# Layer 1 in pairs (0,1) to (6,7) and block 8 as two half blocks, with an unread weight quarter left unwritten and a ring of seven weight tiles

## The chip, the core and the metric

The kernel runs on one core of a Trainium2 chip. The metric is the device time of the run in microseconds (us); the median of three runs is taken. TensorE (PE) does the matrix products, VectorE (DVE) and ScalarE (ACT) the elementwise work, GpSimd (POOL) almost nothing, and SyncE (SP) issues nearly all transfers (DMA), in the order of its program.

## The reference

4608 tokens of 512 values go through three steps. First a linear attention: for each of 8 batches of 576 tokens and 8 heads, `kv = k^T v`, `out = q kv`, divided by its root mean square and scaled. Then layer 1, a gated feed-forward with an inner width of 1536, and layer 2, one with a squared ReLU and an inner width of 2048:

```python
xn = x / rms(x) * rms_g
h1 = silu(xn @ w_gate) * (xn @ w_val)      # 512 -> 1536
x2 = h1 @ w_out                            # 1536 -> 512
h2 = maximum(x2 @ w_in, 0) ** 2            # 512 -> 2048
out = h2 @ w_out2                          # 2048 -> 512
```

All is float32; the weights arrive as float64.

## The kernel before

**Blocks and stages.** The tokens are cut into 9 blocks of 512 (`T`). `stages` (L341) lists what is worked on together: in layer 1 the blocks (0,1), then (2,) alone, then (3,4), (5,6), (7,8); in layer 2 (0,1) to (6,7) and at last (8,8), which is block 8 as two half blocks of 256 columns (`width`, L100). Each stage has an x part (`x_stage`, L741: the products with w_gate and w_val, or w_in) and an h part (`h_stage`, L848: the products with w_out or w_out2).

**Products.** Each float32 operand is split into a high part (ACT, L624) and a low part (DVE, L625), and a product is three passes of matmuls (`PASSES`, L712). A pair of blocks can go through a scheme with seven products of quarter matrices in place of eight (`run_seven` L963, the second half of `x_stage`), which needs sums of weight quarters (S1 to S4, made once) and sums of the data quarters (T1 to T4: `x_steps` L639, and `forms` L856 with their subtractions L628). The other way is plain (`run_plain` L933, L794). `x_plain` (L344) makes the x part plain in (0,1) and (2,); `h_plain` (L333) makes the h part plain in (0,1), (2,), (3,4). A matmul of L717 (x part), L945 (plain h) or L980 (seven, h) takes a 128x128 weight tile against 512 columns, or 256 in a half-block stage. One product of an x part for one pair of weight tiles is 12 matmuls, six for each half of the pair (`g`); so is one product of an h part (`d`).

**Counts of matmuls.** x part of layer 1: 288 for a plain block, 504 for a pair (or for two half blocks) with seven products. h part of layer 1: 144 for a plain block, 252 for a pair with seven products. Layer 2: 336 and 336 for a pair.

**Weights.** In stage (0,1) the weights are turned from float64 to split float32 and put into DRAM (`prep_unit` L122: `hi` L190, `lo` L201, `put` L211). A tile in DRAM (`wd`) has four quarters of both halves of a pair; the tile h=0 has the quarters 11, 12, 21, 22, the tile h=1 the sums S1 to S4. Units of kind "words" make the h=0 part, units of kind "sums" load the words again (L176) and make the h=1 part, and units of kind "all" (layer 2) make both. Steps of these units stand in `prep_q`; `tick` (L690), called after every six matmuls of an x part, takes `pace["prep"]` of them (L1187). From the second stage on each product loads its weights, 128 x 2 x 2 x 256 float32 = 0.524 MB, into one of the tiles of a ring (`w_fetch` L359, `W_RING` = 5, four more in layer 2). SP issues the next load once the product has given its tile free, so SP goes in step with PE.

**Order.** All instructions stand in an order written out by hand: `after(n, ...)` and `at(t, ...)` put work on a later tick, each engine takes its instructions in that order. Three operand tiles (`hop`) hold the split operands of the h part; `ahead` forms the operand of product n+2 when product n is put out. The queue `xs` (L876 to L918) holds what the next stage's x part needs: loads of x (L668), scaling (layer 1, L674), splits and subtractions, one item per call of `x_next`, which in `run_seven` stands after each six matmuls. `h_result` (L1021) writes the results of layer 1 into tiles `o` of the pool `t` (8 tiles in rotation, L77) and puts them to `x2d` five ticks later. The attention of blocks 2 to 8 is spread over the ticks of layer 1 (`kv_events` L580, `o_events` L586, L764 to L773).

## Time and profile before

| | us |
|---|---|
| median of three runs (1625.38 to 1630.46) | 1626.92 |
| the profiled execution | 1629.3 |
| its span, first to last instruction | 1627.5 |
| PE busy | 1598.4 (98%) |
| DVE busy | 1152.8 (71%) |
| ACT busy | 715.0 (44%) |
| DMA q1, share of 16 engines | 82.3% |

The stages of the profiled execution, read from the chain that ended last: (0,1) to 264.5, (2,) to 381.5, (3,4) to 581.2, (5,6) to 757.4, (7,8) to 930.9, then layer 2 with (0,1) to 1084.2, three more pairs to 1541.2, and (8,8) to 1621.9. The granted clock of TensorE is 0.998 of its full 2.4 GHz in the mean. A busy share near 100% on PE tells that little time is left between matmuls, so what counts is how much work PE has and where it waits.

### The profile page before, as it was taken

The page shows a single profiled execution, that of the slowest core. Times are in us where ns is not written, and L with a number is a line of the kernel's source. Part 1 is how long each engine was busy: PE and PEld are TensorE (multiplying, and loading weights), DVE is VectorE, ACT ScalarE, POOL GpSimd, SP SyncE. Part 2 cuts the span into 40 slices and gives each one's busy share as a digit, 9 for nine tenths or more (in the row PEclk, how much of TensorE's full clock was granted, in tenths as well). Part 3 has the DMA queues.
Part 4 walks back from the last instruction along what each step waited for, and adds up shares of the span by engine and source line. Part 5 has one row for each costly group of instructions (what it writes and reads, how often), then busy time and mean ns, then how long its engine had stood idle before and what let it go on. Part 6 is the DMA issues. An engine that isn't in the chain of part 4 may idle for free.

```text
span 1627.5 us, 21390 instructions
## 1 busy us (share of the span) xinstructions
PE 1598.4 (98%) x8024; PEld 1327.2 (82%) x8024; DVE 1152.8 (71%) x1590; ACT 715.0 (44%) x967; POOL 6.7 (0%) x19
## 2 busy tenths in 40 slices
PE   8899999999999999999999999999999999999998
PEld 7678878777888788788878888888888888888898
DVE  6755675657684767976778688875886588569676
ACT  5543443235553545546554553532353235224433
POOL 0100000000000000000000000000000000000000
PEclk9999999999999999999999999999999999999999
DMA  9885889998997989979997898686678667866797
GB/s 350 284 297 194 274 294 364 381 363 289 365 358 248 351 287 332 367 223 307 356 399 247 286 395 282 222 255 207 196 243 246 196 194 243 244 196 200 225 400 264
DMA packets 176198, 464.92 MB, mean 286 GB/s; under 512 B 14048, under 2 KB 47840, under 8 KB 171744
## 3 DMA queue, kind: packets, MB, share of 16 engines
q1 hardware_dynamic: 175552, 463.30, 82.3%
q8 instruction: 64, 1.05, 0.3%
q10 hardware_dynamic: 544, 0.26, 0.1%
q14 instruction: 38, 0.31, 0.0%
HBM read 356.55 MB, written 106.95 MB: 285 GB/s over the span
## 4 chain that ended last, share of the span: by engine, by line
PE 83%; DMA 6%; DVE 5%; ACT 3%; issue 1%; SPq 0%; POOL 0%; POOLq 0%; ACTq 0%; DVEq 0%
PE c L717 45%; PE a L980 16%; PE e L980 8%; PE acc L945 8%; PE d L980 4%; DMA wt<-wd_g 2%; DMA wd_p<-ws 2%; DMA kvraw<-in_kv_dram 1%; PE ops L448 1%; PE kvps L408 1%; DVE wpw L169 1%; DVE ws L202 1%; ACT ws L199 1%; DVE wpw L163 1%; ACT wpw L157 1%
## 5 line engine op out<-in xcount | busy, mean ns | idle before, releaser
L717 PE MATMUL c<-xo,wt 128*128 128x512 f32 (+1 forms) x3480 | 765.2, 380 | 7.9 <-DMA wt<-wd_g 6.1
L717 PEld LDWEIGHTS c<-xo,wt 128*128 128x128 f32 x3480 | 627.6, 188 | 135.0 <-DMA wt<-wd_g 5.9
L625 DVE TENSOR_TENSOR ho<-hr,ho 128x1024 fp32r<-128x1024 f32 (+1 forms) x212 | 243.0, 1147 | 86.7 <-ACT ho L624 85.8
L624 ACT ACTIVATE ho<-hr 128x1024 fp32r<-128x1024 f32 (+1 forms) x212 | 212.0, 1001 | 184.9 <-PE a L980 85.9
L980 PE MATMUL a<-ho,wt 128*128 128x512 f32 (+1 forms) x1248 | 267.0, 373 | 0.0
L980 PEld LDWEIGHTS a<-ho,wt 128*128 128x128 f32 x1248 | 221.6, 188 | 41.1
L728 ACT ACTIVATE s<-c 128x512 f32<-128x512 f32 (+1 forms) x228 | 127.7, 573 | 175.0 <-PE c L717 174.5
L732 DVE TENSOR_TENSOR c<-c,s 128x512 f32<-128x512 f32 (+1 forms) x174 | 112.8, 649 | 80.2 <-PE c L717 77.2
L717 PE MATMUL c<-xo,ws 128*128 128x512 f32 x576 | 139.8, 398 | 4.3 <-ACT ws L199 3.6
L980 PE MATMUL e<-ho,wt 128*128 128x512 f32 (+1 forms) x624 | 133.5, 373 | 0.0
L717 PEld LDWEIGHTS c<-xo,ws 128*128 128x128 f32 x576 | 106.8, 189 | 28.7 <-ACT ws L199 4.8
L980 PEld LDWEIGHTS e<-ho,wt 128*128 128x128 f32 x624 | 110.8, 188 | 20.6
L628 DVE TENSOR_TENSOR hr<-hr 128x1024 f32<-128x1024 f32 (+1 forms) x104 | 118.5, 1139 | 1.8
L625 DVE TENSOR_TENSOR xo<-xr,xo 128x1024 fp32r<-128x1024 f32 (+1 forms) x58 | 67.0, 1157 | 57.2 <-ACT xo L624 57.2
L945 PE MATMUL acc<-ho,wt 128*128 128x512 f32 x432 | 102.9, 396 | 1.9 <-DMA wt<-wd_o 1.9
L788 DVE TENSOR_TENSOR hr<-c,hr 128x512 f32<-128x512 f32 x108 | 73.8, 685 | 33.4 <-PE c L717 30.8
L945 PEld LDWEIGHTS acc<-ho,wt 128*128 128x128 f32 x432 | 81.4, 191 | 19.5 <-DMA wt<-wd_o 2.3
L202 DVE TENSOR_TENSOR ws<-wpl,ws 128x1024 fp32r<-128x1024 f32 x49 | 59.8, 1220 | 28.9 <-ACT ws L199 28.8
L739 DVE SCALAR_TENSOR_TENSOR hr<-c 128x512 f32<-128x512 f32 (+1 forms) x120 | 76.5, 638 | 3.6
L199 ACT ACTIVATE ws<-wpl 128x1024 fp32r<-128x1024 f32 x49 | 51.7, 1055 | 44.8 <-DVE wpl L188 23.6
L624 ACT ACTIVATE xo<-xr 128x1024 fp32r<-128x1024 f32 (+1 forms) x58 | 57.1, 1002 | 32.0 <-DVE xr L628 32.0
L783 ACT ACTIVATE r<-c 128x512 f32<-128x512 f32 (+1 forms) x40 | 22.1, 554 | 108.1 <-PE c L717 98.5
(81 smaller groups left out, 1148.9 us busy)
## 6 DMA issues: line engine op xcount, KB each, us to landing
wt<-wd_g SPq DMA_DIRECT2D x150, 512.0 KB, 6.8
wt<-wd_i SPq DMA_DIRECT2D x140, 512.0 KB, 5.0
wt<-wd_p SPq DMA_DIRECT2D x140, 512.0 KB, 3.9
wt<-wd_o SPq DMA_DIRECT2D x78, 512.0 KB, 5.1
wd_g<-ws SPq DMA_DIRECT2D x24, 1024.0 KB, 10.0
kvraw<-in_kv_dram SPq DMA_DIRECT2D x32, 512.0 KB, 7.1
wd_i<-ws SPq DMA_DIRECT2D x16, 1024.0 KB, 7.9
wd_p<-ws SPq DMA_DIRECT2D x16, 1024.0 KB, 8.5
```

Source lines behind the costliest of these rows:

```text
L199: nc.scalar.activation(out=st[h][:, :, 0, :], in_=quarters(st["sw"[1 - h]]), func=AF.Copy)
L202: nc.vector.tensor_tensor(out=st[h][:, :, 1, :], in0=quarters(st["sw"[1 - h]]), in1=st[h][:, :, 0, :].bitcast(F32), op=ALU.subtract,)
L624: nc.scalar.activation(out=dst[:, 0], in_=src, func=AF.Copy)
L625: eng.tensor_tensor(out=dst[:, 1], in0=src, in1=dst[:, 0].bitcast(F32), op=ALU.subtract)
L628: eng.tensor_tensor(out=o, in0=x, in1=y, op=ALU.subtract)
L717: nc.tensor.matmul(ps, lhsT=w[:, a, kc * 128:(kc + 1) * 128], rhs=x[:, b, kc, :], start=(start and n == 0 and kc == 0), stop=(n == 2 and k ...
L728: nc.scalar.activation(out=t, in_=ps, func=AF.Copy)
L732: nc.vector.tensor_tensor(out=o, in0=ps, in1=t, op=ALU.add)
L739: nc.vector.scalar_tensor_tensor(out=hr, in0=c, scalar=0.0, in1=c, op0=ALU.max, op1=ALU.mult)
L788: after(2, lambda: nc.vector.tensor_tensor(out=hr, in0=c, in1=hr, op=ALU.mult))
L945: nc.tensor.matmul(acc[c], lhsT=wt[:, a, (c % 2) * 128:(c % 2 + 1) * 128], rhs=x[:, b, e, :], start=(n == 0 and e == 0 and a + b == 0), st ...
L980: nc.tensor.matmul(ps, lhsT=w[e][:, a, d * 128:(d + 1) * 128], rhs=x[:, b, e, :], start=(i in (1, 2, 5) and q == 0 and e == 0 and a + b == 0),
```

## The change

Layer 1 has the stages (0,1), (2,3), (4,5), (6,7) and (8,8), where (8,8) is block 8 as two half blocks, as layer 2 had already. All of them but (0,1) have an x part with seven products; the h part is plain in (0,1) and (2,3). So stage (0,1) now loads and prepares the x of two blocks (2 and 3) and has to finish their attention, whose events are put closer together. In the tiles h=0 the quarters 22 and 21 change places (on the host too), so that 21 is the last; it isn't read by seven products. It is not put to DRAM for w_gate, w_val, w_in and w_out2, and not computed either for the last two (`n_hi`, `n_put`). Two tiles of the pool `sm` join the ring after stage (0,1): seven tiles in layer 1, eleven in layer 2. The units of layer 2's weights are spread as 2, 4, 6, 0 over the stages of layer 1 from (2,3) to (8,8), and 4 in the first stage of layer 2, where it was 4, 3, 6 and 3; seven "sums" units of w_gate and w_val stand in the x part of (2,3), where they stood in that of (2,). A result tile of a half block waits until its other half is there.

```diff
@@ -31,8 +31,8 @@
-PLACE_X = {"11": (0, 0), "12": (0, 1), "21": (0, 2), "22": (0, 3)}
-PLACE_H = {"11": (0, 0), "21": (0, 1), "12": (0, 2), "22": (0, 3)}
+PLACE_X = {"11": (0, 0), "12": (0, 1), "22": (0, 2), "21": (0, 3)}
+PLACE_H = {"11": (0, 0), "22": (0, 1), "12": (0, 2), "21": (0, 3)}
...
@@ -72,7 +72,7 @@
-    smp = ctx.enter_context(tc.tile_pool(name="sm", bufs=1))
+    smp = ctx.enter_context(tc.tile_pool(name="sm", bufs=2))
...
@@ -127,6 +127,7 @@
+        n_hi, n_put = (3 if m in "ip" else 4), (4 if m == "o" else 3)
...
@@ -196,20 +197,23 @@
-            nc.scalar.activation(out=st[h][:, :, 0, :], in_=quarters(st["sw"[1 - h]]), func=AF.Copy)
+            k = 4 if h else n_hi
+            nc.scalar.activation(out=st[h][:, :k, 0, :], in_=quarters(st["sw"[1 - h]])[:, :k], func=AF.Copy)
 
         def lo(h):
+            k = 4 if h else n_hi
             nc.vector.tensor_tensor(
-                out=st[h][:, :, 1, :],
-                in0=quarters(st["sw"[1 - h]]),
-                in1=st[h][:, :, 0, :].bitcast(F32),
+                out=st[h][:, :k, 1, :],
+                in0=quarters(st["sw"[1 - h]])[:, :k],
+                in1=st[h][:, :k, 0, :].bitcast(F32),
...
         def put(h):
-            nc.sync.dma_start(out=wd[pair][h][:, :, e], in_=st.pop(h).bitcast(F32))
+            k = 4 if h else n_put
+            nc.sync.dma_start(out=wd[pair][h][:, :k, e], in_=st.pop(h)[:, :k].bitcast(F32))
...
@@ -331,23 +335,24 @@
     def h_plain(layer, blocks):
-        return len(blocks) == 1 or layer == 1 and blocks[0] < 5
+        return layer == 1 and blocks[0] < 4
-    stages = [(1, (0, 1)), (1, (2,))] + [(1, (n, n + 1)) for n in range(3, NB, 2)]
-    stages += [(2, (n, n + 1)) for n in range(0, NB - 1, 2)] + [(2, (NB - 1, NB - 1))]
+    stages = [
+        (layer, b) for layer in (1, 2) for b in [(n, n + 1) for n in range(0, NB - 1, 2)] + [(NB - 1, NB - 1)]
+    ]
     def x_plain(layer, blocks):
-        return len(blocks) == 1 or (layer, blocks) == stages[0]
+        return (layer, blocks) == stages[0]
...
@@ -603,9 +608,9 @@
-                at(u + 4 + 4 * c, lambda c=c: att_y(j, c, nc.vector))
-                at(u + 6 + 4 * c, lambda c=c: x1_turn(j, c))
-                at(u + 22 + 2 * c, lambda c=c: x1_put(j, c))
+                at(u + 4 + every * c, lambda c=c: att_y(j, c, nc.vector))
+                at(u + 4 + every // 2 + every * c, lambda c=c: x1_turn(j, c))
+                at(u + 4 + every // 2 + every * NQ + every // 2 * c, lambda c=c: x1_put(j, c))
...
@@ -665,7 +668,9 @@
-        nc.sync.dma_start(out=t, in_=x1d[j][k].rearrange("c p t -> p c t") if layer == 1 else x2d[j][:, k, cols])
+        nc.sync.dma_start(
+            out=t, in_=x1d[j][k, :, cols].rearrange("c p t -> p c t") if layer == 1 else x2d[j][:, k, cols]
+        )
...
@@ -756,21 +761,20 @@
             if first[0] and (n, t) == (0, 2):
                 while chain:
                     tick()
                 t0 = now[0] + 1
-                for j in range(stages[1][1][0], NB):
-                    gap, period = (6, 47) if j < 5 else (8, 60)
-                    if j == 2:
-                        kv_events(j, t0, gap)
-                        t0 += 28
-                    o_events(j, t0, 5)
+                kv_events(2, t0, 4)
+                t0 += 18
+                for j in range(2, NB):
+                    gap = 4 if j == 2 else 8
+                    o_events(j, t0, 5, every=2 if j < 4 else 4)
                     if j + 1 < B:
-                        kv_events(j + 1, t0 + 17, gap)
-                    t0 += period
+                        kv_events(j + 1, t0 + 17, 6 if j == 3 else gap)
+                    t0 += (35, 44, 55)[min(j - 2, 2)]
...
@@ -876,20 +880,13 @@
-            if first[0]:
-                at = {"11": (0, "11"), "21": (0, "21")}
-                when = dict.fromkeys(at, 11)
-            elif len(blocks) == 1:
-                at = {"11": (1, "12"), "21": (1, "22"), "12": (2, "12"), "22": (2, "22")}
-                when = dict.fromkeys(at, 0)
-            elif plain:
+            if plain:
                 at = {"11": (1, "11"), "21": (2, "11"), "12": (1, "21"), "22": (2, "21")}
                 when = {"11": len(seq), "21": len(seq), "12": len(seq) + 2, "22": len(seq) + 2}
             else:
                 at = {"11": (1, "11"), "21": (2, "11"), "12": (1, "12"), "22": (2, "12")}
                 when = {"11": 4 * nq, "21": 4 * nq, "12": 5 * nq, "22": 5 * nq}
-            if len(nb) == 1:
-                at = {b: at[b] for b in ("11", "21")}
+
...
@@ -909,11 +906,14 @@
-            t1 = when["11"]
-            load_two(t1, "11", "21", 4 if nl == 1 else 3)
-            xs.extend([step(0, t1), step(1, t1)])
-            if len(nb) > 1:
-                t2 = when["12"]
+            t1, t2 = when["11"], when["12"]
+            if first[0]:
+                xs.extend([load("11"), load("21"), load("12"), load("22")] + [(t2, [])] * 3)
+                xs.extend((t2, [lambda n=n: x_scale(xt[n], n)]) for n in ("11", "21", "12", "22"))
+                xs.extend(step(n, 13 if n > 6 else 11) for n in range(8))
+            else:
+                load_two(t1, "11", "21", 4 if nl == 1 else 3)
+                xs.extend([step(0, t1), step(1, t1)])
                 load_two(t2, "12", "22", 3 if nl == 1 else 2)
                 xs.extend(step(n, t2) for n in range(2, 8))
...
@@ -1013,7 +1013,7 @@
-            if nxt and len(nxt[1]) > 1:
+            if nxt:
                 late.extend([lambda n=n: x_step(n) for n in range(8, 13)])
...
@@ -1022,17 +1022,28 @@
-        j, o = blocks[n], new_tmp("o")
+        j, parts = blocks[n], T // width(blocks)
+        o = o_two.pop(c, None)
+        if o is None:
+            o, whole = tmp.tile([128, T], F32, tag="t", name="o"), parts == 1
+            if not whole:
+                o_two[c] = o
+        else:
+            whole = True
         to = o
         if turned(j):
-            to = o.rearrange("p (i a t) -> p a i t", a=NQ, t=BL)
-            ps, t = (x if x is None else x.rearrange("p (a i t) -> p a i t", a=NQ, t=BL) for x in (ps, t))
+            k = NQ // parts
+            a = slice(n * k, (n + 1) * k) if parts > 1 else slice(0, NQ)
+            to = o.rearrange("p (i a t) -> p a i t", a=NQ, t=BL)[:, a]
+            ps, t = (x if x is None else x.rearrange("p (a i t) -> p a i t", a=k, t=BL) for x in (ps, t))
         if t is not None:
             add(to, ps, t)
         else:
             nc.scalar.activation(out=to, in_=ps, func=AF.Copy)
-        after(5, lambda: nc.sync.dma_start(out=x2d[j][:, c, :], in_=o))
-
+        if whole:
+            after(5, lambda: nc.sync.dma_start(out=x2d[j][:, c, :], in_=o))
...
@@ -1080,24 +1091,25 @@
-            + prep_units([(key, "sums") for key in gv[:N_SUMS]], 6, hops, rooms + [(xop, "x21"), (smp, "sm")] * 2, stgs),
-            prep_units([(key, "sums") for key in gv[N_SUMS:]], 5, hops, xts[:3], stgs + xts[:2:-1]),
+            + prep_units([(key, "sums") for key in gv[:N_SUMS]], 6, hops, rooms + [(smp, "sm", smp, "sm")], stgs),
-        for n, many in enumerate((4, 3, 6, 3)):
+        for n, many in enumerate((2, 4, 6, 0, 4), 1):
             units = l2_units[lo:lo + many]
             lo += many
-            if n == 3:
+            if n == 5:
                 preps.append(units)
                 continue
-            steps = prep_units(units, 11 if many < 5 else 9, hops, hops, stgs, pad=True)
+            steps = prep_units(units, 11 if many < 5 else 9, hops, hops, stgs, pad=True) if many else []
             if n == 1:
+                steps = prep_units([(key, "sums") for key in gv[N_SUMS:]], 4, hops, hops, stgs, pad=True) + steps
+            if n == 2:
                 steps = prep_units(o_sums[3:], 9, hops, hops, stgs, pad=True) + steps
             preps.append(steps)
-        h_preps[2] = prep_units(o_sums[:3], 9, hops, [(xop, "x22"), (xop, "xT4")], stgs, pad=True)
+        h_preps[1] = prep_units(o_sums[:3], 9, hops, [(xop, "x22"), (xop, "xT4")], stgs, pad=True)
...
@@ -1184,7 +1196,7 @@
-            pace["prep"] = 1.0 if n == 0 else len(prep_q) / {1: 40, 4: 70, 5: 40}.get(n, 64)
+            pace["prep"] = 1.0 if n == 0 else len(prep_q) / {1: 62, 2: 66, 3: 70}.get(n, 46)
...
@@ -1196,7 +1208,8 @@
-                for _ in range(W_RING):
+                w_places.extendleft([(smp, "sm")] * 2)
+                for _ in range(len(w_places)):
                     w_fetch()
...
@@ -1216,10 +1229,11 @@
-        return rows(w)
-    def rows(w):
-        return np.ascontiguousarray(w.reshape(-1, 2, 128, DM).transpose(0, 2, 1, 3)).view(np.int64)
+        return rows(w, (0, 1, 3, 2))
+    def rows(w, order=(0, 3, 2, 1)):
+        w = w.reshape(-1, 2, 128, 2, DM // 2).transpose(0, 2, 1, 3, 4).reshape(-1, 128, 4, DM // 2)
+        return np.ascontiguousarray(w[:, :, order, :]).reshape(-1, 128, 2, DM).view(np.int64)
```

## Rows read from the trace of the kernel before

**Rows 1.** The profile page: engine, busy us, share of the span, instructions.
```profile
PE 1598.4 (98%) x8024; PEld 1327.2 (82%) x8024; DVE 1152.8 (71%) x1590; ACT 715.0 (44%) x967; POOL 6.7 (0%) x19
```

**Rows 2.** Waits of PE: line, what it waited for, us in total, times, longest.
```profile
PE c L717 <- DMA wt<-wd_g: 6.1, 6, 1.7
...
PE acc L945 <- DMA wt<-wd_o: 1.9, 1, 1.9
```

**Rows 3.** The chain that ended last, in order of time: start us, us, what.
```profile
554.80 26.37 PE acc L945 x108
...
1236.52 76.16 PE c L717 x336
...
1541.16 40.37 PE c L717 x336
```

**Rows 4.** Stretches of layer 1: us, then each engine's busy us, PEclk, DMA share, GB/s.
```profile
264.50:304.00 39.50, 37.74 (x194) 31.14 (x193) 20.20 (x38) 11.19 (x18) 0.00 (x0) 1.00 1.01 355
304.00:344.00 40.00, 36.68 (x208) 28.49 (x207) 24.26 (x50) 10.60 (x14) 0.00 (x0) 1.00 1.02 378
...
815.00:874.00 59.00, 57.84 (x253) 46.80 (x252) 43.09 (x60) 30.86 (x45) 0.00 (x0) 1.00 0.97 369
```

**Rows 5.** The same view around the wait in the plain h part of (3,4).
```profile
550.00:554.50 4.50, 2.89 (x24) 1.90 (x22) 2.59 (x3) 3.10 (x5) 0.00 (x0) 1.00 1.01 380
554.50:558.00 3.50, 3.20 (x8) 2.52 (x9) 1.89 (x3) 1.54 (x2) 0.00 (x0) 0.56 1.05 413
```

**Rows 6.** The same view over the half-block stage of layer 2: x part, h part.
```profile
1541.00:1581.50 40.50, 40.50 (x339) 40.48 (x338) 27.17 (x65) 14.16 (x36) 0.00 (x0) 1.00 1.03 385
1581.50:1622.00 40.50, 40.37 (x337) 40.16 (x335) 31.21 (x56) 18.66 (x33) 0.00 (x0) 1.00 0.84 305
```

**Rows 7.** PE groups by shape: xcount, busy us, mean ns, idle before.
```profile
L717 PE MATMUL c<-xo,wt 128*128 128x512 f32 x3144 | 724.6, 391 | 7.9 <-DMA wt<-wd_g 6.1 <-DVE hr L732 0.8 <-DVE c L732 0.6
...
L945 PE MATMUL acc<-ho,wt 128*128 128x512 f32 x432 | 102.9, 396 | 1.9 <-DMA wt<-wd_o 1.9
```

**Rows 8.** DMA in the x part of (2,), 264.5 to 344: all, and issues to landing.
```profile
DMA packets 12315, 29.13 MB, mean 366 GB/s; under 512 B 863, under 2 KB 2911, under 8 KB 12309
...
wt<-wd_g SPq DMA_DIRECT2D x19, 512.0 KB, 9.2
wd_g<-ws SPq DMA_DIRECT2D x7, 1024.0 KB, 9.6
```

**Rows 9.** DMA in the x part of (3,4), 381.5 to 508.
```profile
DMA packets 15636, 41.43 MB, mean 328 GB/s; under 512 B 1190, under 2 KB 3824, under 8 KB 15115
```

**Rows 10.** DMA in the x part of (7,8), 757.5 to 874.
```profile
DMA packets 13595, 41.67 MB, mean 358 GB/s; under 512 B 1003, under 2 KB 1003, under 8 KB 12819
```

**Rows 11.** Instructions at the start of (7,8), in order of time.
```profile
760.69 0.61 SPq L1034 DMA_DIRECT2D x2d<-o  x1
```

**Rows 12.** DMA in the h part of (7,8), 874 to 931: us to landing.
```profile
xr<-x2d SPq DMA_DIRECT2D x4, 512.0 KB, 6.2
...
x2d<-o SPq DMA_DIRECT2D x6, 256.0 KB, 6.0
```

**Rows 13.** Instructions in that h part, in order of time: start us, us.
```profile
898.50 1.22 DVE L628 TENSOR_TENSOR hr<-hr 128x1024 f32<-128x1024 f32 x1
...
899.80 2.93 SPq L668 DMA_DIRECT2D xr<-x2d  x2
...
907.06 1.05 ACT L624 ACTIVATE xo<-xr 128x1024 fp32r<-128x1024 f32 x1
...
909.29 1.22 DVE L625 TENSOR_TENSOR ho<-hr,ho 128x1024 fp32r<-128x1024 f32 x1
...
910.42 1.22 DVE L625 TENSOR_TENSOR xo<-xr,xo 128x1024 fp32r<-128x1024 f32 x1
```

**Rows 14.** DVE groups by shape: xcount, busy us, mean ns, idle before.
```profile
L625 DVE TENSOR_TENSOR ho<-hr,ho 128x512 fp32r<-128x512 f32 x28 | 19.1, 684 | 6.4 <-ACT ho L624 5.7
...
L732 DVE TENSOR_TENSOR c<-c,s 128x256 f32<-128x256 f32 x24 | 10.1, 419 | 9.5 <-PE c L717 9.5
```

More of the change, by code (lines that the diff above doesn't have):

```diff
@@ L933, in run_plain @@
         def run_plain():
-            for nb, j in enumerate(blocks):
+            for nb in range(len(blocks)):
                 bk = [banks.popleft() for _ in range(4)]
```

13 lines of the change are left out of this document (6 added, 7 removed).

## The prediction

> **What bounds the kernel now.** The page first: PE is busy for 98% of the span, DVE for 71%, ACT for 44% [rows 1]. So time goes with the work of PE, and with the few waits of PE. The list of waits comes next: 6.1 us for weights of w_gate and w_val and 1.9 us for weights of w_out are the large ones after the start [rows 2]. The chain gives the price of a matmul where nothing disturbs it: 336 with 512 columns in 76.16 us are 226.7 ns each, 336 with 256 columns in 40.37 us are 120.1 ns each [rows 3]. Half the columns cost 53% and not 50%: half-width matmuls pay 6.8 ns more than half a full one. The stretches show where PE waits in layer 1: it lacks 1.76 and 3.32 us in the two halves of the x part of (2,), with the DMA share at 1.01 and 1.02, and 1.16 us in (7,8) at 0.97 [rows 4]. So these waits are for transfers in crowded stretches. One more lies in the plain h part of (3,4): PE is busy for 2.89 of 4.5 us, and in the next 3.5 us the granted clock is 0.56 of full speed, a mix of its two levels, 1.2 and 2.4 GHz [rows 5]. The 108 matmuls from there took 26.37 us in place of 24.5, so this wait of 1.9 us cost 1.9 us more by the clock [rows 2, 3]. The stage whose form the change copies, (8,8) of layer 2, holds PE without a gap while DMA moves 385 GB/s, and its h part has DVE busy for 31.2 of 40.5 us [rows 6].
>
> **PE's work.** Behind stage (0,1), layer 1 has x parts of 288 + 3 x 504 = 1800 and plain and seven h parts of 144 + 288 + 2 x 252 = 936 full matmuls. The groups agree: 3144 - 4 x 336 = 1800, and 432 = 144 + 288 [rows 7]. That is 2736 x 226.7 ns = 620.2 us. After: 3 x 504 + 288 + 2 x 252 = 2304 full ones, 522.3 us, and 504 + 252 = 756 half ones, 90.8 us; sum 613.1. **PE gains 7.1 us.** The attention's matmuls keep their number and only move to earlier ticks.
>
> In the TensorE: Matmul & The Clock Gate page of the Trainium skill (section Back-to-back issue gap) a warm matmul takes N/2.4 + 2.5 ns, 215.8 and 109.2 here; by that the gain would be 10.7 us and the sum 3.6 us lower. The trace disagrees, with 226.7 and 120.1 ns [rows 3].
>
> **The x part of (2,3).** It replaces that of (2,) as the place where seven "sums" units run beside the weight stream. The (2,) part moved 29.13 MB in 79.5 us at 366 GB/s, seven puts of 1.05 MB among them, a weight load landing 9.2 us after its issue [rows 8]. Without its 5.1 us of lacking PE time it would have asked for 392 GB/s. In (2,3): 42 loads x 0.524 = 22.0 MB, sums 7 x (0.524 + 1.049) = 11.0, two "all" units (1.049 in, 0.786 + 1.049 out) 5.8, attention and results about 7 (the 41.43 MB of (3,4) less 43 loads and four units of 3.15 leave 6.3, and blocks now come a little closer) [rows 9]. That is 45.8 MB; the x part of (3,4) took 126.5 us [rows 9], so 364 GB/s, but the sums stand in the first 48 of 84 ticks: 12.6 + 11.0 + 4 MB in some 72 us, 383 GB/s. The ask is the old one, and the two more tiles are 1.05 MB, 2.9 us at 366 GB/s. Bounds for the wait: 2.6 us (5.5, the old one for 72 us, less 2.9) to 6.1 (the ring lends nothing), and 13.6 if the stretch gets only the 328 GB/s of (3,4) [rows 9]. I take 3.5, nearer to the low end because the demand falls behind tick 48 and the ring can refill. **-2.6 us.** Behind a load that waits on SP for its put stand all later loads, puts and attention loads.
>
> **The h part of (2,3)** is that of (3,4) with the same three o units. Its wait of 1.9 + 1.9 us arose because SP put o's weights late; two tiles more are 2 x 2.72 us more lead. **-3.5 us** (0 to -3.8). For the same reason the 1.16 us of (7,8), whose units also write 0.26 MB less each [rows 4]: **-0.9** (0 to -1.2). The unread quarter saves 12 + 16 puts of 0.26 MB and a quarter of 16 `hi` and `lo`; it lies beside PE and I give it no time of its own. If the transfers were the bound it would be 7.3 MB, 20 us at 366 GB/s, against 27 more weight loads (255 for 228), 14.2 MB.
>
> **The x part of the half stage.** 42 loads of 0.524 MB in 60.5 us are 364 GB/s, below the 385 shown [rows 6], with a ring of seven for nine there. I give 0.5 (0 to 5). Then the tiles `o`: the last results of (6,7) are put late, the first of the two at +3.3 us in the old order (760.69, the stage beginning at 757.4) [rows 11], where SP follows a full product; with half products about +1.8. It lands 6.0 us later [rows 12], at 7.8. The tile is wanted by the seventh new tile, the copy of product 5, at 5.8, and PE needs this copy at 7.9: late by some 0.5, and by 3 with a landing of 9 us. I give 1.5. Together **+2** (0 to 6).
>
> **The h part of the half stage**, the largest new term. A product lasts 12 x 120.1 ns = 1.44 us. The next stage's x is full width and its steps stand at fixed counts of products, from product 9 on, so all distances halve. In the old (7,8) the first x load waits for a subtraction of DVE, is issued at 899.80, and its split starts at 907.06, 7.3 us later, more than the 6.2 it takes to land [rows 12, 13]. Counted from the start of product 9, the half stage has the two loads at 0.8 and 2.4, landing at 7.0 and 8.6; the split stands at 4.7. ACT waits, and the form of operand 14 behind it comes too late for product 14, due at 7.2. From 8.1 (7.0 + 1.05 on ACT) DVE still has 7 forms, 4 full splits, 2 full subtractions, 4 half adds. Full ones follow each other in 1.13 us (909.29, 910.42), 0.09 less than they are long [rows 13]; so 0.60 for a form of 0.68 and 0.34 for an add of 0.42 [rows 14]: 4.2 + 6.8 + 1.4 = 12.4. The last operand is there at 20.5, its product ends at 21.9; undisturbed it ends at 17.3. That is 4.7, and 0.5 for handing from ACT to DVE: **+5.2 us**. Low end 1 (loads land in time and the operand tiles cover DVE's surplus), high end 10 (landing 9.2 [rows 8] and once more 1.9 of clock).
>
> **The rest.** The first stage of layer 2 gets four units for three, 2.1 MB more, 5.7 us of transfer at 366 GB/s [rows 8], beside a deeper ring: **+1** (0 to 3). Stage (0,1): SP waits for the put of block 3's x, some 8 us, ahead of the loads of the sums units; DVE gets two splits and two subtractions more. Operands are formed two products (11 us) ahead: **+1** (-1 to 4).
>
> **The sum.** -7.1 - 2.6 - 3.5 - 0.9 + 2 + 5.2 + 1 + 1 = -4.9 us. The profiled run took 1629.3 (span 1627.5), 2.4 above the median of 1626.9; so 1624.4 for such a run and 1622 for the median.
>
> **Rivals.** *Covered*: the loads of x land in time and the ring swallows the waits: -7.1 - 6.1 - 3.8 - 1.2 + 2.4 (DVE's surplus in the half stage) = -15.8, 1611. For it: (8,8) of layer 2 had no wait with DVE at 0.77; against: that stage has no next one. *Transfers bound (2,3)*: at 328 GB/s its 45.8 MB take 139.6 us, 13.6 of waiting for my 3.5, and 1.9 of clock: +7.1 us, 1634. It gives slower from a rate under 333 GB/s on (a wait over 11.5 us). For it: shares of 1.01 and 1.02 in (2,) [rows 4]; against: 366 GB/s there [rows 8], 358 in (7,8) [rows 10]. *The ring does nothing*: crowded transfers are late whatever the depth, 6.1 and 3.8 us stay: +1.2, 1628.
>
> The DMA: Bandwidth & Descriptors page of the Trainium skill (Specifications) states an HBM limit of about 358 GB/s for a core. By that the second rival would hold, (2,3) taking 127.9 us and the 33.0 MB of the half stage 92.3 for 90.8. The trace disagrees, with 385 GB/s over 40 us [rows 6].
>
> **How the numbers follow.** My forecast has a chance of 0.52, with 1616 to 1628 as its own range; covered 0.22; transfers bound 0.18; ring does nothing 0.08. A measurement tells 0.3%, 4.9 us, from no change: below 1622.0 is faster, above 1631.8 slower. Half of the forecast (0.26) and "covered" are faster, 0.48; the other half, the last rival and 0.02 of the third are the same, 0.36; the rest, 0.16, slower. The range reaches from the second case to the third: 1611 to 1634.
>
> **What would show it.** Right: 504 and 252 half-width matmuls of L717 and L980 in layer 1 at 120 ns each, with no gap between them in the x part; waits of ACT or DVE for x from x2d shortly before layer 2, and PE lacking about 5 us there; fewer waits for wt<-wd_o. Wrong: no such lack (then nearer 1611), or PE lacking over 10 us in the x part of (2,3), or in stage (0,1), whose end should lie within 5 us of 264.5 plus the attention moved into it.

## The result and the profile after

| | before | after |
|---|---|---|
| median, us | 1626.94 (1625.38 to 1630.46) | 1645.28 (1643.29 to 1647.51) |
| ratio to before, 95% interval | | 1.0110 (1.0087 to 1.0133) |
| span of the profiled execution, us | 1627.5 | 1645.0 |
| mean granted clock | 0.998 | 0.993 |

The change makes the kernel 18 us slower, against a forecast of 5 us faster. The page of the kernel after: busy us and share of each engine, then the transfers.

```profile
PE 1602.0 (97%) x8348; PEld 1342.5 (82%) x8348; DVE 1183.4 (72%) x1680; ACT 735.7 (45%) x1043; POOL 6.7 (0%) x19
...
q1 hardware_dynamic: 176400, 470.12, 82.4%
...
HBM read 370.71 MB, written 99.61 MB: 286 GB/s over the span
```

PE is busy for 3.6 us more, though its work fell, and the time in which it does nothing grew from 29.1 to 43.0 us [rows 1]. The work did fall as forecast. In the chain of after, the x part of the half stage stands as one piece without a gap:

```profile
842.19 60.47 PE c L722 x504
...
1254.17 76.16 PE c L722 x336
```

That is 120.0 ns for a half matmul, and 226.7 for a full one as before [rows 3]. So the gain of 7.1 us is there, and some 25 us (these 7.1 and the 17.5 by which the span grew) came in elsewhere: 13.9 as idle time of PE, and about 10.7, an estimate from the busy time (3.6 more for 7.1 less), as matmuls that ran longer at a lower clock (0.993 for 0.998 in the mean). The list of waits of PE (what for, us in total, times, longest) says for whom:

```profile
PE c L722 <- ACT s L733: 8.3, 6, 3.0
PE acc L945 <- ACT ws L201: 3.8, 1, 3.8
...
PE a L980 <- ACT ho L629: 2.6, 1, 2.6
PE a L980 <- DVE ho L630: 2.4, 3, 1.0
PE c L722 <- DVE c L737: 2.4, 3, 1.3
PE kvps L413 <- DVE ss L488: 2.2, 1, 2.2
```

No wait of PE for a streamed weight tile (`wt`) is left in it; 6.1 and 1.9 us of those are gone [rows 2]. In their place stand waits for ACT and DVE. The stretches place them (us, then busy us of PE, PEld, DVE, ACT, POOL; PEclk, DMA share, GB/s). After: h part of (0,1); x and h part of (4,5); x part of (6,7); x and h part of the half stage; first x part of layer 2.

```profile
195.50:280.60 85.10, 78.36 (x402) 63.18 (x401) 63.40 (x102) 42.80 (x53) 0.00 (x0) 0.94 0.90 315
...
481.00:607.50 126.50, 123.70 (x594) 101.91 (x593) 99.47 (x163) 66.07 (x102) 0.00 (x0) 1.00 0.94 339
607.50:667.40 59.90, 58.76 (x254) 46.67 (x253) 52.93 (x68) 32.43 (x39) 0.00 (x0) 1.00 0.76 256
667.40:784.90 117.50, 115.29 (x505) 94.27 (x504) 84.32 (x117) 63.98 (x92) 0.00 (x0) 1.00 0.95 344
...
842.00:902.50 60.50, 60.50 (x506) 60.47 (x504) 30.30 (x69) 26.63 (x67) 0.00 (x0) 1.00 0.99 364
902.50:940.60 38.10, 32.97 (x254) 31.95 (x253) 29.12 (x43) 17.67 (x30) 0.00 (x0) 0.96 0.99 363
940.60:1025.50 84.90, 79.33 (x338) 63.79 (x337) 67.80 (x95) 38.27 (x53) 0.00 (x0) 0.98 0.95 349
```

The same view of the kernel before: h part of (0,1), x and h part of the plain (2,), x part of (5,6), first x part of layer 2.

```profile
189.70:264.40 74.70, 74.06 (x410) 59.73 (x409) 55.71 (x87) 37.75 (x46) 0.00 (x0) 1.00 0.91 325
264.40:344.00 79.60, 74.52 (x401) 59.73 (x400) 44.46 (x87) 21.79 (x32) 0.00 (x0) 1.00 1.02 366
344.00:381.50 37.50, 37.50 (x202) 30.98 (x201) 18.39 (x22) 17.76 (x26) 0.00 (x0) 1.00 0.91 325
...
581.20:700.30 119.10, 118.34 (x537) 97.76 (x537) 88.90 (x145) 60.11 (x90) 0.00 (x0) 1.00 0.94 335
...
930.90:1007.90 77.00, 76.72 (x338) 62.88 (x337) 63.01 (x87) 35.23 (x49) 0.00 (x0) 1.00 0.95 353
```

Stage (0,1) ends at 280.6 for 264.5, 16.1 us later. About 4 us of it is attention that moved in: 48 matmuls more on PE in that stage, four steps `ops` and one `kvps` of later blocks. In its h part (85.1 us for 74.7) PE stands idle for 6.7 us where it was 0.6, and the matmuls run at a clock of 0.94 for 1.00. Layer 1 behind it takes 660.0 us for 666.4. The first stage of layer 2 takes 84.9 for 77.0. From there on both kernels take 619 us. 16.1 - 6.4 + 7.9 = 17.6, the growth of the span.

Two places show how PE is held up. First, stage (0,1): DVE's list, then ACT and PE, in the order of time (start us, us, what; in brackets the idle time before it and who ended it).

```profile
219.53 1.18 DVE L164 SCALAR_TENSOR_TENSOR wpw<-wps,wpw 128x1024 int32<-128x1024 int32 x1
220.64 0.68 DVE L541 TENSOR_TENSOR y<-y,r 128x512 f32<-128x512 f32 x1
221.24 1.22 DVE L170 SCALAR_TENSOR_TENSOR wpw<-wps,wpw 128x1024 int32<-128x1024 int32 x1
...
222.49 1.06 ACT L201 ACTIVATE ws<-wpw 128x1024 fp32r<-128x1024 f32 x1 [4.36 <-DVE wpw L170]
223.60 0.50 PE L945 MATMUL acc<-ho,ws 128*128 128x512 f32 x1 [3.82 <-ACT ws L201]
```

L164 and L170 turn the words of a weight that PE needs next; L541 scales the attention's `y` and was written between them, and one more pair of attention steps (L541, L556) ran just ahead, from 218.18 to 219.53. DVE takes its list in order, so ACT gets the weight late and PE stands for 3.82 us. The pair ahead takes 1.35 us and L541 between the two steps 0.60: together about half of the wait. The stretches there:

```profile
219.80:223.60 3.80, 0.00 (x1) 0.00 (x1) 3.30 (x5) 1.11 (x2) 0.00 (x0) 1.00 0.97 369
223.60:227.00 3.40, 2.64 (x19) 1.62 (x19) 3.37 (x4) 1.84 (x2) 0.00 (x0) 0.65 0.60 235
227.00:230.00 3.00, 3.00 (x11) 2.36 (x8) 1.39 (x2) 0.00 (x0) 0.00 (x0) 0.50 1.01 301
```

The granted clock is 0.65 and 0.50 of full speed behind the wait (0.50 is the lower level, 1.2 GHz), and 36 matmuls from 227.07 take 10.50 us where the same number took 8.46 at 203.0. At 271.39 PE waits once more, 2.16 us for the attention's sums (L488), which stand in DVE's list behind steps on weights (L205, L189) and on the next stage's x (L630).

Second, the h part of the half stage, in the same view:

```profile
916.73 1.54 SPq L671 DMA_DIRECT2D xr<-x2d  x2
...
923.85 1.06 ACT L629 ACTIVATE xo<-xr 128x1024 fp32r<-128x1024 f32 x1 [3.49 <-DMA xr<-x2d]
924.81 0.61 ACT L629 ACTIVATE ho<-hr 128x512 fp32r<-128x512 f32 x1
925.48 0.50 PE L980 MATMUL a<-ho,wt 128*128 128x256 f32 x2 [2.65 <-ACT ho L629]
...
926.82 1.77 PE L980 MATMUL a<-ho,wt 128*128 128x256 f32 x10 [0.84 <-DVE ho L630]
...
939.36 1.45 PE L980 MATMUL a<-ho,wt 128*128 128x256 f32 x10 [0.98 <-DVE ho L630]
```

ACT waits for the x of layer 2, the operand behind it in its list is late, and then DVE gives the pace.

### The profile page after: what moved, and what is told of

Its sections match the earlier page's. It is cut to its first block, busy times and chain, and to the rows that moved or that the text cites. A ratio compares the mean times of both kernels' runs of the same rounds, so it can differ in the third digit from the quotient of the medians.

```text
span 1645.0 us, 22390 instructions
## 1 busy us (share of the span) xinstructions
PE 1602.0 (97%) x8348; PEld 1342.5 (82%) x8348; DVE 1183.4 (72%) x1680; ACT 735.7 (45%) x1043; POOL 6.7 (0%) x19
## 4 chain that ended last, share of the span: by engine, by line
PE 56%; DVE 5%; DMA 3%; ACT 1%; issue 1%; SPq 0%; ACTq 0%; DVEq 0%
PE c L722 29%; PE a L980 16%; PE e L980 8%; PE d L980 4%; DMA wd_p<-ws 1%; DVE ho L630 1%; DMA wraw<-in_wo_dram 1%; DMA xr<-x2d 1%; ACT ws L201 1%; DVE ws L205 1%; DMA wd_i<-ws 1%; DVE hr L633 1%; DVE wpl L189 0%; DVE c L737 0%; DVE hr L737 0%
## 5 line engine op out<-in xcount | busy, mean ns | idle before, releaser
L630 DVE TENSOR_TENSOR ho<-hr,ho 128x1024 fp32r<-128x1024 f32 (+1 forms) x227 | 249.9, 1103 | 83.8 <-ACT ho L629 82.8
L980 PE MATMUL a<-ho,wt 128*128 128x512 f32 (+1 forms) x1392 | 287.2, 364 | 5.1 <-ACT ho L629 2.6
L980 PEld LDWEIGHTS a<-ho,wt 128*128 128x128 f32 x1392 | 239.3, 189 | 48.3 <-DVE ho L630 4.5
L733 ACT ACTIVATE s<-c 128x512 f32<-128x512 f32 (+1 forms) x264 | 140.2, 546 | 163.7 <-PE c L722 163.3
L980 PE MATMUL e<-ho,wt 128*128 128x512 f32 (+1 forms) x696 | 144.4, 367 | 1.1 <-DVE ho L630 1.1
L980 PEld LDWEIGHTS e<-ho,wt 128*128 128x128 f32 x696 | 120.6, 191 | 22.7 <-DVE ho L630 2.2
L630 DVE TENSOR_TENSOR xo<-xr,xo 128x1024 fp32r<-128x1024 f32 (+1 forms) x63 | 69.3, 1103 | 64.7 <-ACT xo L629 64.7
L792 DVE TENSOR_TENSOR hr<-c,hr 128x512 f32<-128x512 f32 (+1 forms) x120 | 75.8, 632 | 30.1 <-PE c L722 27.2
L741 ACT ACTIVATE hr<-hr 128x512 f32<-128x512 f32 (+1 forms) x72 | 41.6, 578 | 96.0 <-DVE hr L737 96.0
L205 DVE TENSOR_TENSOR ws<-wpl,ws 128x1024 fp32r<-128x1024 f32 (+1 forms) x45 | 50.7, 1126 | 43.8 <-ACT ws L201 43.8
L945 PE MATMUL acc<-ho,ws 128*128 128x512 f32 x288 | 72.7, 410 | 4.6 <-ACT ws L201 3.8
L737 DVE TENSOR_TENSOR hr<-c,s 128x512 f32<-128x512 f32 (+1 forms) x72 | 44.6, 619 | 40.7 <-PE c L722 40.5
L201 ACT ACTIVATE ws<-wpl 128x1024 fp32r<-128x1024 f32 (+1 forms) x45 | 44.1, 980 | 64.2 <-DVE wpl L189 26.4
```

The costliest lines, as they stand in the source:

```text
L201: nc.scalar.activation(out=st[h][:, :k, 0, :], in_=quarters(st["sw"[1 - h]])[:, :k], func=AF.Copy)
L205: nc.vector.tensor_tensor(out=st[h][:, :k, 1, :], in0=quarters(st["sw"[1 - h]])[:, :k], in1=st[h][:, :k, 0, :].bitcast(F32), op=ALU.subtract,)
L630: eng.tensor_tensor(out=dst[:, 1], in0=src, in1=dst[:, 0].bitcast(F32), op=ALU.subtract)
L733: nc.scalar.activation(out=t, in_=ps, func=AF.Copy)
L737: nc.vector.tensor_tensor(out=o, in0=ps, in1=t, op=ALU.add)
L792: after(2, lambda: nc.vector.tensor_tensor(out=hr, in0=c, in1=hr, op=ALU.mult))
```

## The experiments

All times are medians with the ratio to the kernel before and its 95% interval. The kernel before was run again beside each (its medians are 1626.5 to 1630.0), so totals are compared by the ratios. The times of stages are from the profiled execution. Where the edit is to the kernel after, "after" is 1645.28 (1.0110), with the stages shown above.

**The good parts alone.** The kernel before with the ring of seven (its pool `sm` cut in two tiles; the core of the edit is shown), and the kernel after with the `extendleft` line left out:

```diff
-                for _ in range(W_RING):
+                w_places.extendleft([(smp, "sm")] * 2)
+                for _ in range(len(w_places)):
```

> The kernel before with the ring of seven tiles (eleven in layer 2) and nothing else of the change; the pool sm is cut into two tiles for it. PE waits 6.1 us for weights in (2,), 1.9 (and 1.9 by the clock) in (3,4) and 1.1 in (7,8) in the kernel before. If the two tiles give the lead that these waits lack, (2,) falls from 117.1 to 113 or less, (3,4) from 199.5 to 196, (7,8) by 1, the whole by 6 to 9. If transfers are late whatever the depth, all stay, and the whole within 2 us of before.

> The changed kernel with the ring of five tiles (nine in layer 2). If the ring is worth what the prediction gave it, (2,3) takes 6 us more than its 200.4, and the half-block stage, which uses 0.524 MB every 1.44 us, some us more than its 98.6, with PE waiting for wt. If depth does nothing, (2,3) stays within 1 us and the half-block stage within 2.

Before with the ring: 1620.95 (0.9941, 0.9923 to 0.9960). The x part of (2,) falls from 79.6 to 73.1 us, the h part of (3,4) from 73.9 to 70.1; the stretches of these two:

```profile
265.10:338.10 73.00, 73.00 (x401) 59.91 (x400) 44.49 (x87) 21.92 (x32) 0.00 (x0) 1.00 1.04 396
501.30:571.40 70.10, 70.10 (x346) 57.99 (x345) 43.51 (x69) 30.11 (x41) 0.00 (x0) 1.00 0.91 323
```

PE is busy throughout both stretches, with 396 GB/s in the first. But the x part of (7,8), expected to fall by 1, takes 118.9 us for 116.4: its wait for weights (1.1 us) is gone, and one of 1.8 us for ACT stands in its place. After without the ring: 1660.71 (1.0189, 1.0159 to 1.0220); (2,3) takes 210.4 us for 200.4, the half stage 102.7 for 98.6, and waits for `wt<-wd_g` are back with 7.0 us and for `wt<-wd_o` with 4.5. The ring is worth 7 us by the spans and 9 by the medians taken side by side in the old order, and 12 to 13 in the new one.

**The unwritten quarter.** After with all quarters computed and written (shown), and before with the ring of seven in which the unread quarter of w_in and w_out2 alone is neither computed nor written:

```diff
-        n_hi, n_put = (3 if m in "ip" else 4), (4 if m == "o" else 3)
+        n_hi, n_put = 4, 4
```

> The changed kernel with all four quarters computed and written. 28 puts get 0.26 MB back (7.3 MB), and 16 hi and lo a third more (some 0.3 us each on ACT and DVE). If the saved quarter is hidden, as the prediction has it, the whole stays within 2 us of 1645; if transfers hold the stages (0,1) to (6,7), it takes 5 to 20 us more, spread over them; if DVE does, some 3 to 5 us in (4,5), (6,7) and the first stage of layer 2.

> The kernel before with the ring of seven tiles and with the unread quarter of w_in and w_out2 neither computed nor written; the stages stay as before. The ring alone gave a ratio of 0.994. The quarter saves 16 puts of 0.26 MB and some 0.3 us each on ACT and DVE for 16 high and low parts. Undoing the whole saving in the changed kernel cost 5 us in the profile, most in (2,3), (4,5) and the first of layer 2. If the saving holds here too, (7,8) falls by 1 to 2.5 and the whole by 1 to 4 against the ring alone; if it is hidden, it stays within 1 us of it.

With all quarters: 1652.47 (1.0137, 1.0108 to 1.0165), span 1650.2 for 1645.0, with some 2.4 us more in each of the x parts of (2,3) and (4,5) and 1.2 in the first stage of layer 2. No wait of PE for a weight tile comes back; the waits that grew in the two x parts are those for ACT in (2,3) (1.5 to 2.7 us) and for DVE in (4,5) (2.8 to 3.5), with a clock of 0.99 in both. Before with ring and quarter: 1616.28 (0.9921, 0.9906 to 0.9936), the lowest ratio of all. Its span is 1615.1: 5.2 us under that with the ring alone, 12.4 under the kernel before and 29.9 under the kernel after. In it the x part of (7,8) takes 115.3 us for 116.4, the first stage of layer 2 76.5.

**Attention elsewhere in stage (0,1).** Two edits to the kernel after: the attention of block 4 and later put 26 ticks later, and blocks 2 and 3 put earlier (the second line, with gaps of 3 ticks for 4 in the events of block 2).

```diff
-                    t0 += (35, 44, 55)[min(j - 2, 2)]
+                    t0 += (35, 70, 55)[min(j - 2, 2)]
...
+                    t0 += (31, 52, 55)[min(j - 2, 2)]
```

> The attention of block 4 and all that follows it starts 26 ticks later, so block 4 leaves stage (0,1) and most of block 8 leaves (4,5). In the changed kernel stage (0,1) ends at 280.6, (4,5) takes 186.4 and (6,7) 174.6. If DVE, crowded by attention, is what makes PE wait in (0,1) at 269 and in (4,5), the end of (0,1) comes to about 272 (4.0 of attention moved on, 2.2 of waiting and 1.9 of clock gone), (4,5) to about 179, (2,3) and (6,7) get 4 each, and the whole falls by 6 to 8, to about 1638. If the weights' preparation is the cause, attention only changes its place: the whole stays within 2 us of 1645. The wait for w_out at 220 stays in both.

> The key-value products of blocks 2 and 3 follow each other every three ticks in place of four, so block 3's scaling and turning on DVE come eight ticks earlier and no longer lie among the last words units of w_out; block 4 keeps its place. Stage (0,1) ends at 280.6 in the changed kernel. If these DVE steps between the words steps are what delays w_out (PE waits 3.8 and 0.8 us and loses 2.1 to the clock at 220), it ends at about 274 and the whole at about 1639. If the words units are late by their own chain of ACT and DVE, it stays at 279 to 282; key-value loads that come too slowly would add to it.

Later: 1654.67 (1.0155, 1.0140 to 1.0170). The h part of (0,1) falls from 85.1 to 76.4, but (2,3) goes from 200.4 to 209.3 and (4,5) from 186.4 to 195.3. Earlier: 1647.84 (1.0113, 1.0098 to 1.0128). The wait at 220 shrinks, and this one takes its place:

```profile
273.31 1.12 PE L413 MATMUL kvps<-kvraw 128*64 128x64 f32 x16 [5.09 <-DVE ss L488]
```

Both expectations of a gain were wrong: in both places tried, the loss came back in the same stage or in the next ones.

**Less for DVE.** After, with the sums of squares of the attention replaced by a constant and `y` not scaled, for blocks 2 to 8:

```diff
+            if j > 1:
+                for t in ss_t[j]:
+                    nc.vector.memset(t, 64.0)
...
     def att_sum(i, n):
         j, c = divmod(i, NQ)
+        if j > 1:
+            return
...
     def att_y(j, c, eng):
+        if j > 1:
+            return
```

> The changed kernel, with part of the attention's DVE work left out for blocks 2 to 8: the sums of squares are a constant and y is not scaled, so the output is not that of the reference. 12 DVE instructions of some 0.69 us fall away per block (8 sums, 4 scalings), 58 us of DVE in all; matmuls, transfers and the preparation of weights stay. Theory: DVE, at 75 to 88% in the stages up to the first of layer 2 and in its written order, is what now holds PE in (0,1), (4,5) and (2,3), since the plain stage (2,) with DVE at 54% is gone. Then the h part of (0,1) falls from 85.1 to 76 or less, the x part of (4,5) from 126.5 to 123, its h part from 59.9 to 57.5, the whole by 12 to 16. Rival: the transfers and the pace of the weights' preparation hold PE; then these stages stay within 2 us, the whole within 3 of 1645. The half-block stage (38.1) and the first stage of layer 2 (84.9) have no attention and stay in both.

1634.92 (1.0029, 1.0012 to 1.0045), the span 13.3 us shorter than after. Its stretches for the h part of (0,1) and the first stage of layer 2:

```profile
195.90:271.50 75.60, 73.59 (x401) 59.87 (x400) 54.98 (x91) 42.28 (x52) 0.00 (x0) 1.00 0.95 335
...
926.90:1012.30 85.40, 79.27 (x337) 63.71 (x337) 67.81 (x95) 38.33 (x53) 0.00 (x0) 0.98 0.95 349
```

The first falls from 85.1 to 75.6, PE's lack from 6.7 to 2.0, and the clock is whole; the wait at 220 falls from 3.82 to 1.24 us and the one at 271 is gone. (4,5) falls from 186.4 to 182.1, but (2,3), which the theory named too, takes 201.8 for 200.4. The half stage and layer 2 are as in after, as expected, since no attention is left there. So most of what stage (0,1) and (4,5) lost hangs on these attention steps. The kernel before was not run without them; it had little to gain there, as PE lacks 0.6 us in its h part of (0,1) and 0.8 in (5,6). The run doesn't tell the steps' amount from their place in the order.

**Amount or place.** The kernel before with ring and quarter, and 32 multiplications of a scratch tile by itself on DVE (the expectations below call them additions; 0.42 us each, 13.4 in all, nothing uses them), spread over one part of a stage (the core is shown; in (5,6) the pace is 0.4 for 0.67):

```diff
     def tick():
         now[0] += 1
+        pad[1] += pad[0] and 0.67
+        if pad[1] >= 1 and pad[0]:
+            pad[0], pad[1] = pad[0] - 1, pad[1] - 1
+            nc.vector.tensor_tensor(out=scr, in0=scr, in1=scr, op=ALU.mult)
```

> The kernel before with the ring of seven and the unwritten quarter (median 1616.3, x part of (2,) 73.1 us with no wait of PE), and 32 additions on DVE of a scratch tile of 128x256 (0.42 us each, 13.4 us in all, results unused) spread over the ticks of the x part of (2,), which raises its DVE share from 0.61 to 0.79. Theory (the plain stage took side work on DVE without holding PE, and the change removed it): within 1 us of 1616, the x part at 73 to 74. Rival (DVE work costs PE time wherever it stands, about as in stage (0,1) after): +3 to +6 us.

> The same base with the same 32 additions (13.4 us of DVE) spread over the x part of (5,6) (118.6 us, DVE 0.75, to 0.86). Theory (pairs at 0.75 and over have no free place, because operands and sums of products stand in the same list): +3 to +8 us, PE waiting for DVE's and ACT's results there. Rival (only the mean share of DVE counts, and the stage still has 16 us without DVE work): within 1 us of 1616.

> The same base with the same 32 additions (13.4 us of DVE) spread over the h part of (0,1) (74.7 us, DVE 0.75, to 0.92), the place where the change put attention and two more blocks' x. Theory: waits of PE for weights' parts and for the attention's sums as in the kernel after, +4 to +10 us and a lower clock behind them. Rival (the stage (0,1) of after is longer for another reason, as transfers or SP): within 2 us of 1616.

1615.81 (0.9927, 0.9908 to 0.9946) with them in (2,), 1617.97 (0.9940, 0.9921 to 0.9958) in (5,6), 1619.61 (0.9951, 0.9932 to 0.9970) in the h part of (0,1). The padded part takes 73.1 us for 73.1, 120.6 for 118.6, and 77.2 for 74.8. The first and the last of them, by stretches:

```profile
265.00:338.00 73.00, 73.00 (x401) 59.94 (x400) 53.99 (x117) 22.09 (x32) 0.00 (x0) 1.00 1.04 394
```

```profile
191.80:269.00 77.20, 74.11 (x410) 59.77 (x409) 65.71 (x118) 36.90 (x45) 0.00 (x0) 1.00 0.88 306
```

The order of the stages is the theory's: the plain stage takes DVE work for nothing, the other two don't. The size isn't: by the stages 13.4 us cost 2.0 and 2.4 us, under the 3 and 4 that I gave as the least. The ratios of the whole would give about 3 and 5, but their intervals overlap with that of the kernel without padding. In after, DVE has 7.7 us more in the h part of (0,1) than before (63.40 for 55.71), and the part lost 10.4; with the padding DVE has still more there (65.71), and the part takes 77.2 us, where after takes 85.1. So the amount of DVE's work explains little of it. ACT's doesn't either: without the attention's steps on DVE it is the same as in after (42.28 for 42.80 us), and the part takes 75.6. By DVE's groups in this part, 4.9 of the 7.7 us are the two splits and two subtractions of x that the change adds; the attention has 4 scalings and 4 turns in both kernels and 9 sums for 8. So nearly the same attention stands in a fuller list. What is left, by these runs and the two waits shown above, is steps that hand on to each other: attention steps ahead of and between the two halves of a weight that PE waits for, sums that PE waits for behind steps on weights and x. No run moved one such step alone, and none left out the added x steps, so this part is argued.

**GpSimd for DVE.** After, with the scaling of `y` (its edit is `nc.gpsimd` for `nc.vector` in the call of `att_y`) and the quarter sums (L189, shown) on GpSimd.

```diff
-            nc.vector.tensor_tensor(out=of[b], in0=of[x], in1=of[y], op=alu)
+            nc.gpsimd.tensor_tensor(out=of[b], in0=of[x], in1=of[y], op=alu)
```

> The changed kernel with 28 scalings of y (0.68 us each on DVE) and the four quarter sums of each weight unit (0.42 each) on GpSimd in place of DVE: some 19 + 54 us leave DVE, nothing is left out. If DVE's amount in the crowded stages holds PE, as in the run with less DVE work, the h part of (0,1) falls from 85.1 to 78 to 80, (4,5) from 186.4 to 181, the first of layer 2 from 84.9 to 81, the whole by 8 to 14. Against it: GpSimd is slower for an instruction and stands in the chain from words to sums to high part, so the last steps of the units come later; if that decides, (2,3) and the first of layer 2 take 3 to 10 us more and the whole is no faster.

1641.56 (1.0075, 1.0058 to 1.0092): the ratio is 0.35% under that of after, with intervals that overlap, and the profiled span is no shorter (1645.7 for 1645.0), so the 8 to 14 us expected are not shown. The h part of (0,1) takes 84.1 us, not 78 to 80, though DVE is busy in it for 57.7 us in place of 63.4; (4,5) takes 187.1 and the first stage of layer 2 83.7, not 181 and 81. The wait for the weight at 220 is still 3.52 us, though L541 has left DVE's list. DVE at that place, while GpSimd worked on four `y` from 211.03 to 217.87, and then without it:

```profile
212.03 1.95 DVE L170 SCALAR_TENSOR_TENSOR wpw<-wps,wpw 128x1024 int32<-128x1024 int32 x1
...
217.08 1.87 DVE L630 TENSOR_TENSOR ho<-hr,ho 128x1024 fp32r<-128x1024 f32 x1
...
220.72 1.22 DVE L170 SCALAR_TENSOR_TENSOR wpw<-wps,wpw 128x1024 int32<-128x1024 int32 x1
...
224.21 1.22 DVE L630 TENSOR_TENSOR ho<-hr,ho 128x1024 fp32r<-128x1024 f32 x1
```

Steps of 1.22 us with two inputs take 1.87 and 1.95 beside GpSimd; a turn (L556, one input) in the same stretch keeps its 0.70. A quarter sum takes 0.91 us there for 0.42 on DVE. The GPSIMD Engine Reference page of the Trainium skill (section 1. Specifications) says that GpSimd shares its way to the memory with VectorE and contends with instructions that have two inputs there; the trace agrees.

**Units of layer 2's weights.** After had 2, 4, 6, 0 and, in the first stage of layer 2, 4 units. One of the four put into (6,7), one put into the half stage, and the four at another pace (one line each):

```diff
-        for n, many in enumerate((2, 4, 6, 0, 4), 1):
+        for n, many in enumerate((2, 4, 7, 0, 3), 1):
...
+        for n, many in enumerate((2, 4, 6, 1, 3), 1):
...
+            pace["prep"] = 1.0 if n == 0 else len(prep_q) / {1: 62, 2: 66, 3: 70, 5: 36}.get(n, 46)
```

> Units of layer 2's weights spread 2, 4, 7, 0 and 3 in place of 2, 4, 6, 0 and 4: the first stage of layer 2 prepares three as in the kernel before, (6,7) seven. The x part of the first stage of layer 2 takes 84.9 us in the changed kernel and 77.0 before. If the fourth unit is what costs it (its last steps are put out in one burst ahead of the last pair of weights), it falls to 77 to 78 and (6,7) pays at most 2: the whole about 1638. If the late steps of x or the transfers beside the half-block stage cost it, it stays at 82 or more and the whole within 2 us of 1645.

> The kernel after with one of the four units of layer 2's weights taken from the first stage of layer 2 into the x part of the half stage, which has DVE at 0.50 but DMA at 0.99. Theory (a unit costs 5 to 6 us wherever DVE or DMA are full): the first stage of layer 2 falls from 84.9 to about 79, the half stage gains 5 to 8 us with PE waiting for weights (3.1 MB more at 364 GB/s are 8.6 us), total within 3 us of 1645. Rival (only DVE and ACT count): half stage unchanged, total about 1639.

> The changed kernel with the preparation steps in the first stage of layer 2 paced to end 10 ticks earlier. Its x part takes 84.9 us with four units, 78.9 with three. If the burst of left-over steps ahead of the last pair of weights is what PE waits for (3.0 us at 1009 and 2 by the clock), it falls to 80 to 82. If four units are too much for the stage whatever their spacing (their loads and puts must land between steps), it stays at 84 to 86.

1647.16 (1.0100, 1.0083 to 1.0117), 1645.58 (1.0112, 1.0086 to 1.0137) and 1646.75 (1.0105, 1.0087 to 1.0122). The first stage of layer 2 falls from 84.9 to 78.9 and 80.7, but (6,7) goes from 117.5 to 122.6 and the half stage from 60.5 to 65.8, where PE waits 2.7 us for `wt<-wd_g` at a DMA share of 1.00. That (6,7) would pay at most 2 us was wrong. So a unit costs 4 to 6 us in each of these three places: with waits for DVE and ACT in (6,7), with waits for weights in the half stage. The long wait in layer 2's first stage, in the kernel after, comes behind a row of left-over steps of a unit; but the pace alone gives 85.2 for 84.9, so their burst is not what costs the stage its time:

```profile
1006.91 1.06 ACT L201 ACTIVATE ws<-wpl 128x1024 fp32r<-128x1024 f32 x1 [2.73 <-DVE wpl L189]
...
1009.45 5.98 PE L722 MATMUL c<-xo,wt 128*128 128x512 f32 x18 [3.01 <-ACT s L733]
```

**The h part of the half stage.** The split of x put later in the order (first), and the loads put earlier with another order of products (second; only its core is shown):

```diff
-                load_two(t1, "11", "21", 4 if nl == 1 else 3)
+                load_two(t1, "11", "21", 8 if width(blocks) < T else 4 if nl == 1 else 3)
...
+                if half:
+                    when = {"11": 4 * nq - 2, "21": 4 * nq - 1, "12": 5 * nq - 2, "22": 5 * nq - 1}
```

> Five more empty items stand between the loads of the next x and its first split, in the h part of the half-block stage of layer 1 alone, so that the loads have landed when ACT comes to the split. That h part takes 38.1 us in the changed kernel (30.3 without a wait). If ACT's wait for x2d (3.5 us) is what delays the forms, it falls to 31 or 32, and the whole to about 1639. If it is the amount of DVE work behind the loads (12.4 us from the first split on), the wait goes but the work only starts later: 36 to 38, the whole at 1643 to 1645. A mix gives 33 to 36. All other stages stay.

> The changed kernel; in the h part of its half-block stage the products of the groups 6 and 7 take the second and third quarter rows first, so the four loads of the next x leave two products (2.9 us) earlier, and the first split stands 2.2 us later, the first subtraction 0.7 us later. That h part takes 38.1 us (30.3 undisturbed), 35.1 with the split five items later. Theory of wait and amount: no engine waits for x2d any more, and only DVE's surplus stays (12.4 us from the first split at 5.1 us after product 9, so the last product ends some 2 us late): 32 to 33. If the waits were all of it: 30.5. If the amount of DVE were all: 35 or more. The first stage of layer 2 stays at 84 to 86.

Later: 1644.18 (1.0087, 1.0072 to 1.0102); the part falls from 38.1 to 35.1, and the stage behind it rises from 84.9 to 86.0. Earlier: 1644.57 (1.0097, 1.0082 to 1.0112); the part takes 35.7, not the 32 to 33 expected, and the stage behind it 87.3, not 84 to 86, so the two together gain nothing. ACT's waits for x shrink to 0.69 and 1.10 us, and PE waits for weights instead:

```profile
925.76 3.10 PE L994 MATMUL e<-ho,wt 128*128 128x256 f32 x24 [1.15 <-DMA wt<-wd_o]
...
930.32 1.66 PE L994 MATMUL e<-ho,wt 128*128 128x256 f32 x12 [1.46 <-DMA wt<-wd_o]
```

The loads of x that SP issues earlier stand in its list ahead of loads of weights, which now come late.

## Why the prediction was wrong

By its own steps, in us (measured from the profiled executions):

| step | predicted | measured |
|---|---|---|
| PE's work | -7.1 | -7.1: 120.0 and 226.7 ns as priced |
| x part of (2,3) | -2.6 | -3.5: PE lacks 1.6 for 5.1, nothing for weights |
| h part of (2,3) | -3.5 | -3.8: no gap, no lower clock |
| (6,7) for (7,8) | -0.9 | +1.1: lacks 2.2 for 1.1, for ACT and DVE |
| (4,5) for (5,6) | none | +3.1: lacks 3.9 for 0.8 |
| x part of the half stage | +2 | 0 |
| h part of the half stage | +5.2 | +7.8: 38.1 for 30.3 |
| first stage of layer 2 | +1 | +7.9 |
| stage (0,1) | +1 and the attention moved in | +16.1, about 4 of it attention moved in |

With the 4 us of attention that left the later stages these sum to +17.6, by which the span grew.

**Right.** PE's work and the ring: the waits for weights that the ring was to end are gone, and end in the kernel before too when it alone is added; only in (7,8) did a wait for ACT take their place. The size of the ring's term was partly luck: 6.1 us was taken as the wait in (2,), but 1.1 of it stands in (7,8) and was counted there again, so with the 3.5 that it left, -2.6 should have been -1.6. "Transfers bound (2,3)" is refuted at 368 GB/s there, "the ring does nothing" by both ring runs. Two readings under these rivals were off: the x part of (3,4) ends at 507.1 and takes 125.6 us, not 126.5; and 127.9 us for (2,3) are about 2 us of waiting, less than the 3.5 of the forecast, so a rate that gives 127.9 would not make the second rival hold. In the h part of the half stage the order of events is that of the walk: loads late for ACT, then the operand, then DVE. Only the size was off, 7.8 for 5.2: PE stands idle for 5.1 us, as the walk had it, and the other 2.7 are matmuls at the lower clock behind the waits (0.96 in the mean), which only the high end of the term had. The tiles `o` in the x part of the half stage, priced at 1.5 with 0.5 for its loads, cost nothing. The quarter, given no time of its own, is worth 5.2 us by the spans in both orders, though the intervals of the ratios overlap. The waits of PE that grow without it are for ACT and DVE, whose `hi` and `lo` steps it shortens, and not for weights.

**Wrong: the terms "The rest".** Two of them, +1 each, measured +16.1 (12 without the attention moved in) and +7.9, and (4,5) had no term. They were bounded by transfers (5.7 us of loads) and by operands that are formed "two products (11 us) ahead", and no share of DVE in these stages was weighed, only the 71% of the whole span [rows 1]. The runs showed in their place that PE waits for ACT and DVE: in (0,1) 6.7 us of idle PE and the low clock behind it, most of which goes with the attention's steps on DVE, and in the first stage of layer 2 a fourth unit that costs 4 to 6 us. The bounds -1 to 4 and 0 to 3 held no row on what the side work itself needs in its order. In the stretches of before that could be seen: the h part of (0,1) had DVE at 0.75, and the plain (2,) at 0.56 and 0.49. The change takes away a place where side work ran free (13.4 us of padding on DVE for nothing) and puts attention, x and units where the lists of ACT and DVE are close behind PE. The text did name the sign that would show this, stage (0,1) ending more than 5 us past 264.5 plus the attention; it gave it no rival and no chance, and the one rival on the slow side was about transfers.

**What the runs settle.** That the attention's steps on DVE hold PE in (0,1) and (4,5) is shown by leaving them out (13.3 us less span). That a unit costs 4 to 6 us is shown in each of the three stages tried. That the amount of DVE's work alone would cost the h part of (0,1) its time is refuted by the padding. Open: which hand-over counts most (the weight's two steps, the sums that PE waits for, ACT between them, or the added x steps beside the attention), for the runs moved or left out whole groups of steps; and whether the half stage could be had without its 7.8 us, since both orders tried ended between 35 and 36.
